# Attention buffers laid out by last use, and the last rows of v in four DMAs: a fused attention and spectral-mix kernel

## The chip, the cores and the metric

The kernel runs on one core of a Trainium2 chip. The metric is the device time of one execution in microseconds; the figure for the kernel before is the median of three runs.

## The reference

Two computations are chained. The first is sliding-window attention with ALiBi slopes over q, k, v of shape (8 batches, 8 heads, 576 positions, 64):

```python
scores = scale * np.matmul(q, k.transpose(0, 1, 3, 2))
mask = (rel >= 0) & (rel < 128)                # rel = query position - key position
scores = np.where(mask, scores + slopes * -abs(rel), -1e9)
x = softmax(scores) @ v                        # heads side by side: (8, 576, 512)
```

The second mixes x in the frequency domain with a full 512 x 512 complex matrix for each of 64 modes, and adds a channel projection:

```python
X = np.fft.rfft(x, axis=1)
Yr = einsum('bmd,mde->bme', Xr, w_r) - einsum('bmd,mde->bme', Xi, w_i)   # 64 modes
Yi = einsum('bmd,mde->bme', Xr, w_i) + einsum('bmd,mde->bme', Xi, w_r)
y = np.fft.irfft(Y, n=S, axis=1)
u = x + y
return u + np.maximum(u @ w_ch, 0.0)
```

All inputs are FP32. The 128 matrices of w_r and w_i are 134 MB, q, k and v together 28.3 MB.

## The kernel before

**Attention.** The work is cut into 16 units, one for each batch and group of four heads. Its order is written out by hand: the table `STAGE` lists 23 steps with a lag each, and the loop at L541 runs them for one stage after another, so that a stage holds the values of one unit, the scores of another and the casts of a third. For each unit, q, k and v arrive as FP32 in the tiles `qr`, `kr` and `vr`, which hold two units each; `cast` (L225) turns them to BF16 on VectorE (L233, L235 and L238), and at its end calls `load` for the unit two further on. `load` (L198) issues on SP's queue: for v four DMAs of 128 KB, one for each head (L208), and one of 64 KB for the last 64 positions of the four heads, 32 partitions wide (L212); for k and q one DMA of 576 KB each (L219). PE multiplies, ScalarE takes the exponentials into `att` and moves transposed q and k to `qkT`, VectorE masks, and `norm` (L339) divides the values into `x`.

**Semaphores of the DMAs.** The framework keeps eight outstanding DMAs of each kind: an issue on SP waits for the landing of the one eight places before it, and the same holds for the issues of GpSimd (POOL). In the trace, for instance, SP issues at 47.99 us after a landing at 47.97, and at 84.31 after one at 84.25.

**Weights.** GpSimd issues the loads of the weights with a cast to BF16 (512 KB as written for a matrix). Each goes to one of three homes:

- Fourteen matrices go to the pool `early`. From stage 1 to 13 one is let out in a stage, after a copy of one element of `x` (`gate`, L553) that waits for that stage's normalization.
- Seven go over the raw tiles `qr`, `kr` and `vr` as their last contents have been cast (`LATER`, L416 and L556; the issues are recorded at L459). How many in which stage is a small table.
- From L558 on the attention's own pools are closed, and six packs of two matrices go to the pool `wpool`, which lies over the memory that attention held (`load_packs`, L462, issued at L478). Its pack buffers, `YT` and the pool `fin` are laid out over the attention's tiles in the order in which they are allocated, so which tile a pack lies over decides what its DMA waits for. Before them, in GpSimd's order, stands a memset of a part of `YT` (L561).

After that, a matrix is loaded whenever a buffer is freed. The mixing (L858) takes four batches' worth of spectra against each weight; each group of four modes is then scaled (L596) and transposed to `YT`. The inverse transform, the projection and the output (L814 and the store after it) come at the end.

**Tiles of attention.** One pool, `afix`, holds `mask`, `bias`, the two `vb`, the two `vt`, the two `qkT` and the two `att`, in this order; `amid`, allocated before it, holds the cast `q` and `k` and the reciprocals `rec`. The index of `vb`, `vt`, `qkT` and `att` is the unit's number modulo two, so the ones numbered 1 are those of the last unit, 15.

Of the kernel before, what the change touches and what calls it, by code (L numbers as in the profile page):

```python
# [10 lines left out]
FP32 = mybir.dt.float32  # L11
BF16 = mybir.dt.bfloat16
# [8 lines left out]
P = 128  # L21
# [6 lines left out]
FULL = 4  # L28
# [4 lines left out]
W = D + 2  # L33

NC = 24


STAGE = (
# [8 lines left out]
class _Scratch:  # L47


    def __init__(self, ap):  # L50
        self.ap, self.used, self.tags = ap, 0, {}
# [55 lines left out]
class _Attention:  # L107


    def __init__(self, tc, ctx, q, k, v, consts, x, XC, raw):  # L110
        self.tc, self.nc = tc, tc.nc
        self.q, self.k, self.v = q, k, v
        self.ident, self.F, self.FT = consts
        self.x, self.XC = x, XC
        B, H, S, _ = q.shape
        self.S, self.NG = S, H // 4
        self.units = [(b, g) for b in range(B) for g in range(self.NG)]
        self.raw = raw
        self.mid = ctx.enter_context(tc.tile_pool(name="amid", bufs=2))
        self.ps = ctx.enter_context(tc.tile_pool(name="aps", bufs=1, space=PSUM))  # L120
        fix = ctx.enter_context(tc.tile_pool(name="afix", bufs=1))
        self.table = fix.tile([P, H, 2, 2 * P], BF16, name="mask")
        self.bias = fix.tile([P, H, 2, 2 * P], BF16, name="bias")
        self.vb = [fix.tile([P, 2, 4, 2, 2 * W], BF16, name=f"vb{i}") for i in range(2)]
        self.vt = [fix.tile([P, 4, 2, W], BF16, name=f"vt{i}") for i in range(2)]
        self.qkT = [fix.tile([P, 2, 2, (FULL + 1) * P], BF16, name=f"qkT{i}") for i in range(2)]
        self.att = [fix.tile([P, FULL * 8 * P + 64], BF16, name=f"att{i}") for i in range(2)]
        self.loaded, self.casted, self.open = {}, {}, {}

    def fixtures(self, i):  # L130
# [67 lines left out]
    def load(self, w, u):  # L198
        nc = self.nc
        if u >= len(self.units):  # L200
            return
        b, g = self.units[u]
        hs = slice(4 * g, 4 * g + 4)
        if w == "v":
            t = self.raw[w][:, u % 2]
            sv = self.v[b, hs]
            for h in range(4):
                nc.sync.dma_start(  # L208
                    out=t[:, :2, h],
                    in_=sv[h, : FULL * P].rearrange("(r p j) d -> p r (j d)", r=2, j=2),  # L210
                )
            nc.sync.dma_start(  # L212
                out=t[64:96, 2],
                in_=sv[:, FULL * P :].rearrange("h (p j) d -> p h (j d)", j=2),
            )
        else:
            t = self.raw[w][:, u % 2]
            src = (self.q, self.k)["qk".index(w)][b, hs]
            nc.sync.dma_start(  # L219
                out=t.rearrange("p e j d -> p e (j d)"),  # L220
                in_=src.rearrange("(e h) (p j) d -> (h p) e (j d)", h=2, j=TPP),
            )
        self.loaded[w, u] = t
# [115 lines left out]
    def norm(self, u, e):  # L339
        nc = self.nc  # L340
        b, g = self.units[u]
        av = self.open.pop(("av", e, u))
        cs = slice((4 * g + 2 * e) * D, (4 * g + 2 * e + 2) * D)
        rec = self.mid.tile([P, 2, FULL + 1], FP32, tag="rec")
        tiles = av[:, :, : (FULL + 1) * W].rearrange("p h (t n) -> p h t n", n=W)
        nc.vector.reciprocal(rec, tiles[:, :, :, D])
        nc.vector.tensor_tensor(  # L347
            out=self.x[:, b, :, cs].rearrange("p t (h d) -> p h t d", h=2),
            in0=tiles[:, :, :, :D],
            in1=rec.unsqueeze(-1).broadcast_to([P, 2, FULL + 1, D]),  # L350
            op=ALU.mult,
        )
        if b % 2 and g == self.NG - 1 and e == 1:

            nc.vector.tensor_copy(self.x[:64, b, FULL], self.x[:64, b - 1, FULL])
# [21 lines left out]
    def channels(self, u, _):  # L377
# [3 lines left out]
        if g < self.NG - 1:  # L381
            return
        xt = self.open.pop(("xt", u))
        NM = self.F.shape[2] // 2
        view = self.XC[:, : 4 * NC * NM].rearrange(
            "p (q s t b m) -> p q t s b m", q=2, s=3, t=2, b=8)[:, :, :, :, b]
# [13 lines left out]
def kernel(  # L400
# [10 lines left out]
    nc = tc.nc  # L411
# [1 line left out]
    B, H, S, _ = q.shape  # L413
    NM, DM, _ = moe_w_r.shape
    AHEAD = {stage: 1 for stage in range(1, 14)}
    LATER = {13: 2, 14: 2, 15: 3}  # L416
    EARLY, NWA, NWB, AGAIN = 14, 12, 4, 8
    HM = NM // 2

    const = ctx.enter_context(tc.tile_pool(name="const", bufs=1))  # L420
    x = const.tile([P, B, FULL + 1, DM], BF16, name="x")
    XC = const.tile([P, 4 * NC * NM + 16 * NM], BF16, name="XC")
    ident = const.tile([P, P], BF16, name="ident")
# [26 lines left out]
    def load_w(n, pool, chosen=None):  # L450

        for i in ([i for i in todo_w if i not in again][:n] if chosen is None else chosen):
            todo_w.remove(i)
            src = (moe_w_r, moe_w_i)[i % 2][i // 2].rearrange("(p a) e -> p a e", a=4)
            homes[i] = pool
            t = spare.pop(0) if pool is None else pool.tile([P, 4, DM], BF16, tag="w", name="w")
            for part in ((slice(0, 4),) if i < 2 * NM - 1
                         else (slice(0, 2), slice(2, 3), slice(3, 4))):
                nc.gpsimd.dma_start(out=t[:, part], in_=src[:, part])  # L459
            wq[i] = [t[:, a] for a in range(4)]  # L460

    def load_packs(n, pool):  # L462

        for _ in range(n):
            pack = [i for i in todo_w if i not in again][:2]
            if not pack:
                return
            assert len(pack) == 2
            t = pool.tile([P, 2, 4, DM], BF16, tag="w", name="w")
            kinds = {i % 2 for i in pack}  # L470
            for s, i in enumerate(pack):
                todo_w.remove(i)
                homes[i] = pool if s else False
                wq[i] = [t[:, s, a] for a in range(4)]
            m, w = pack[0] // 2, (moe_w_r, moe_w_i)
            if len(kinds) == 1:
                assert pack[1] == pack[0] + 2
                nc.gpsimd.dma_start(  # L478
                    out=t.rearrange("p s a e -> p s (a e)"),
                    in_=w[kinds.pop()][m : m + 2].rearrange("m (p a) e -> p m (a e)", a=4))  # L480
                continue
            for s, i in enumerate(pack):
                src = w[i % 2][i // 2].rearrange("(p a) e -> p a e", a=4)
                for part in ((slice(0, 4),) if i < 2 * NM - 1
                             else (slice(0, 2), slice(2, 3), slice(3, 4))):
                    nc.gpsimd.dma_start(out=t[:, s, part], in_=src[:, part])

    with ExitStack() as actx:
        at = _Attention(tc, actx, q, k, v, (ident, F, FT), x, XC, raw)
# [5 lines left out]
        def run(name, arg, u):  # L495
            if 0 <= u < n and (name, arg, u) not in done:
                done.add((name, arg, u))
                getattr(at, name)(u, arg)
# [6 lines left out]
        table = _forward_table(nc, pool, F, S)  # L505
        next(table)
        nc.vector.memset(norm, 2.0 / S)
        nc.vector.memset(norm[:32], 1.0 / S)
        for t in at.qkT:
# [5 lines left out]
        at.fixtures(1)  # L515
        nc.gpsimd.memset(XC[:, 4 * NC * NM :], 0.0)
        run("cast", "q", 0)
# [23 lines left out]
        for stage in range(min(lags), n + max(lags)):  # L541
            for name, arg, lag in STAGE:
                run(name, arg, stage - lag)
                if name in ("transpose", "exp") and side.get(stage):
                    for _ in range(1 + (name == "transpose")):
                        fn, h = side[stage].pop(0)
# [3 lines left out]
            if stage in AHEAD:  # L550
# [3 lines left out]
                load_w(AHEAD[stage], early)  # L554
            if stage in LATER:
                load_w(LATER[stage], None)  # L556

    with ExitStack() as mctx:  # L558
        fix = mctx.enter_context(tc.tile_pool(name="fix", bufs=1))
        YT = fix.tile([P, 2, 4, B, HM, 2], BF16, name="YT")  # L560
        nc.gpsimd.memset(YT[:, 1, :, :, HM - 4 :], 0.0)  # L561
        pool = mctx.enter_context(tc.tile_pool(name="fin", bufs=2))
        wctx = mctx.enter_context(ExitStack())
        wpool = wctx.enter_context(tc.tile_pool(name="w", bufs=NWA // 2, reuse_waits="tile"))
        again = todo_w[NWA : NWA + AGAIN]
        load_packs(NWA // 2, wpool)
        lctx, pctx = ExitStack(), ExitStack()
        lps = lctx.enter_context(tc.tile_pool(name="lps", bufs=1, side="right", space=PSUM))
        ps = pctx.enter_context(tc.tile_pool(name="fps", bufs=1, space=PSUM))
# [262 lines left out]
        for g in range(NM // 4):  # L832
# [5 lines left out]
            for i in range(8):  # L838
# [14 lines left out]
                for a in range(4):  # L853
                    for t in now:
                        m, ri = t // 2, t % 2
                        c0 = (a // 2 * 2 * NC + 16 * (1 - ri) + a % 2 * 8) * NM + m
                        into = part_acc if g == LAST and m < NM - 1 else acc
# [13 lines left out]
                if k == K1:  # L871
# [15 lines left out]
                    for b in range(2):  # L887
                        nc.gpsimd.dma_start(
                            out=FM.rearrange("(k v) b s -> k v b s", v=16)[:, b, b],
                            in_=FT[64 * b + 56 : 64 * b + 64, b, : 2 * P],  # L890
# [108 lines left out]
```

## Time and profile before

| | |
|---|---|
| median of three runs | 442.07 us (440.07 to 442.46) |
| profiled execution | 440.32 us |
| its span | 438.5 us (1.8 us lie around it) |
| mean granted clock of TensorE | 0.858 |
| busy: PE, VectorE, ScalarE, GpSimd | 73%, 42%, 37%, 20% of the span |
| read from HBM, written | 162.53 MB, 9.44 MB |
| packets of GpSimd's DMA queue | 18992, 67.22 MB as written |
| packets of SP's DMA queue | 33460, 37.79 MB |

Busy shares are means over the whole span. The page also cuts the span into 40 slices of 10.96 us, and gives for each the busy tenths of every engine, the share of time in which the 16 DMA engines worked (a mean over them; overlapping packets can push it a little over 1), and the rate in GB/s as written, so that a weight read in FP32 and written in BF16 counts half of what is read. An engine name with a q behind it (SPq, POOLq) is the queue of instructions of that engine. "A <- B" in a list of waits means that A stood idle until B was done, followed by the microseconds in all, the number of times, and the longest.

### The profile page before, as it was taken

Reading aid. Unit: us, or ns where it says so; the run is one execution under the profiler, and the core shown is the slowest. Engines: PE = TensorE matmul, PEld = TensorE weight load, DVE = VectorE, ACT = ScalarE, POOL = GpSimd, SP = SyncE. Lnnn points to the kernel's source line nnn. Section 1 sums busy time; section 2 is a strip of 40 time slices with the busy share of each in tenths; the row PEclk is TensorE's granted clock in tenths of the full one; section 3 lists DMA queues with packets and bytes.
Section 4 is the critical chain, followed back from the end, with each engine's and each line's share of the span. In section 5 each row is a group of like instructions: output and inputs, shape, how many; then the busy total and the mean of one; then the engine's idle time right before and its main releaser. Section 6 shows DMA issues by size and latency. Waiting matters only on the chain. (4 is left out here: it accounts for less than half of the span.)

```text
span 438.5 us, 8313 instructions
## 1 busy us (share of the span) xinstructions
PE 321.4 (73%) x3509; PEld 179.6 (41%) x3509; DVE 184.4 (42%) x332; ACT 162.1 (37%) x211; POOL 87.9 (20%) x162
## 2 busy tenths in 40 slices
PE   5689899979896534453442487999879999699982
PEld 4357677756665311111111133444434444233430
DVE  7799699987773301010000022322223232122684
ACT  6959799989680000000000012322232323101780
POOL 8711011101215001322112110111111110012500
PEclk9979899999899955555555569999999999989997
DMA  8999999999999999999999999999999999997597
GB/s 284 319 324 309 309 291 306 317 296 301 224 215 185 214 214 214 213 214 214 215 211 215 215 214 214 214 214 215 214 214 214 215 214 214 215 214 150 201 377 296
DMA packets 52489, 105.54 MB, mean 241 GB/s; under 512 B 4052, under 2 KB 23396, under 8 KB 52452
## 3 DMA queue, kind: packets, MB, share of 16 engines
q0 software_dynamic: 18992, 67.22, 76.9%
q1 hardware_dynamic: 33460, 37.79, 26.0%
q8 instruction: 27, 0.44, 0.4%
q14 instruction: 10, 0.08, 0.0%
HBM read 162.53 MB, written 9.44 MB: 392 GB/s over the span
## 5 line engine op out<-in xcount | busy, mean ns | idle before, releaser
L858 PE MATMUL acc<-w,XC 128*32 128x512 bf16 x456 | 79.6, 475 | 71.3 <-DMA w<-in_moe_w_i_dram 35.3
L858 PEld LDWEIGHTS <-XC 128*32 128x32 bf16 x508 | 38.5, 147 | 111.0 <-issue 83.8
L294 ACT ACTIVATE att<-sc 128x1024 bf16<-128x1024 f32 x64 | 64.0, 1032 | 10.6 <-PE sc L284 10.6
L624 ACT CAST ZW<-zw 128x512 bf16<-128x512 f32 x8 | 4.7, 585 | 145.1 <-PE zw L622 145.1
L331 PE MATMUL av<-vb,att 128*128 128x132 bf16 (+1 forms) x576 | 39.0, 219 | 11.2 <-DVE x L347 6.2
L596 DVE TENSOR_SCALAR yq<-acc 128x512 bf16<-128x512 f32 x14 | 9.6, 687 | 83.1 <-PE acc L858 83.1
L331 PEld LDWEIGHTS <-att 128*128 128x128 bf16 x704 | 37.2, 99 | 16.5 <-DVE x L347 10.4
L690 PE MATMUL my<-wch,xT 128*64 128x512 bf16 x288 | 34.5, 381 | 5.8 <-ACT x L721 4.3
L699 ACT CAST XW<-my 128x512 bf16<-128x512 f32 x36 | 19.3, 589 | 49.8 <-PE my L647 49.8
L671 DVE COPY xT<-tr 128x1024 bf16<-128x1024 bf16 x18 | 12.5, 692 | 54.3 <-PE tr L669 54.3
L256 ACT COPY qkT<-tp 128x1152 bf16<-128x1152 bf16 x30 | 33.5, 1116 | 2.4 <-PE tp L250 1.5
L478 POOL DMA_DIRECT2D w<-in_moe_w_i_dram x23 | 16.3, 708 | 66.8 <-PE acc L858 44.1
L478 POOL DMA_DIRECT2D w<-in_moe_w_r_dram x22 | 15.6, 709 | 65.9 <-PE acc L858 48.9
L347 DVE TENSOR_TENSOR x<-av,rec 128x640 bf16<-128x640 f32 x32 | 26.4, 825 | 1.1
L284 PE MATMUL sc<-qkT 64*64 64x256 bf16 (+2 forms) x640 | 25.2, 265 | 2.1 <-ACT qkT L256 1.2
L690 PEld LDWEIGHTS <-xT 128*64 128x64 bf16 x288 | 17.2, 109 | 21.6 <-issue 9.2
L814 DVE TENSOR_TENSOR o<-yy,r 128x1024 f32<-128x1024 f32 (+1 forms) x22 | 21.6, 1026 | 4.8 <-DMA Z<-yq 2.6
L553 POOL COPY gate<-x 1x1 bf16<-1x1 bf16 x13 | 6.3, 482 | 83.3 <-DVE x L347 83.3
L233 DVE CAST vb<-vr 64x1024 bf16<-64x1024 f32 x32 | 22.6, 707 | 0.2
L284 PEld LDWEIGHTS <-qkT 64*64 64x64 bf16 x640 | 14.6, 110 | 19.7 <-issue 16.7
L721 ACT CAST x<-my 128x512 bf16<-128x512 f32 x18 | 10.5, 585 | 32.0 <-PE my L647 32.0
L271 PE MATMUL sc<-bias,ident 128*128 128x512 bf16 x64 | 21.2, 415 | 1.4 <-ACT att L294 1.4
(134 smaller groups left out, 435.6 us busy)
## 6 DMA issues: line engine op xcount, KB each, us to landing
w<-in_moe_w_i_dram POOLq DMA_DIRECT2D x23, 1024.0 KB, 35.8
w<-in_moe_w_r_dram POOLq DMA_DIRECT2D x22, 1024.0 KB, 35.7
qr<-in_q_dram SPq DMA_DIRECT2D x16, 576.0 KB, 9.1
kr<-in_k_dram SPq DMA_DIRECT2D x16, 576.0 KB, 6.8
vr<-in_v_dram SPq DMA_DIRECT2D x64, 128.0 KB, 7.0
w<-in_moe_w_r_dram POOLq DMA_DIRECT2D x16, 512.0 KB, 14.3
w<-in_moe_w_i_dram POOLq DMA_DIRECT2D x13, 512.0 KB, 24.0
out_dram<-o SPq DMA_DIRECT2D x13, 512.0 KB, 4.6
```

The lines of the kernel that those rows point to most:

```text
L233: nc.vector.tensor_copy(self.vb[u % 2][row, :, :, :, W * half : W * half + D], src[row, :2])
L256: (self.nc.vector.tensor_copy if u < 2 and w == "q" else self.nc.scalar.copy)(dst.rearrange("q h (p j) -> q h p j", j=TPP), tp.rearrange(" ...
L271: nc.tensor.matmul(sc[:, e], lhsT=self.ident, rhs=self.bias[:, hv].rearrange("p j n -> p (j n)"), start=True, stop=False, skip_group_check ...
L284: nc.tensor.matmul(sc[64 * half : 64 * half + 64, e, j * 256 + c0 : j * 256 + c0 + n], lhsT=qkT[row, 1, h, k0 + j : k0 + P : 2], rhs=qkT[r ...
L294: self.nc.scalar.activation(self.att[u % 2][:, kt * 8 * P : (kt + 1) * 8 * P], sc.rearrange("p e n -> p (e n)"), AF.Exp, scale=1.0 / math. ...
L331: nc.tensor.matmul(bank[:, qt * W : qt * W + rhs[j].shape[1]], lhsT=att[:, o : o + P], rhs=rhs[j], start=(n == 0 and j == 0), stop=(n == l ...
L347: nc.vector.tensor_tensor(out=self.x[:, b, :, cs].rearrange("p t (h d) -> p h t d", h=2), in0=tiles[:, :, :, :D], in1=rec.unsqueeze(-1).br ...
L478: nc.gpsimd.dma_start(out=t.rearrange("p s a e -> p s (a e)"), in_=w[kinds.pop()][m : m + 2].rearrange("m (p a) e -> p m (a e)", a=4))
L690: nc.tensor.matmul(mm[ROWS[half]], lhsT=lhsT, rhs=wch[:, dt], start=(dt == 0), stop=False, skip_group_check=True,)
L699: nc.scalar.copy(XW[:, j, n], mms[n])
L814: nc.vector.tensor_tensor(out=o[:, c], in0=yy[:, c], in1=r[:, c], op=ALU.add)
L858: nc.tensor.matmul(into[32 * (m % 4) : 32 * (m % 4) + 32], lhsT=XC[:, c0 : c0 + 31 * NM + 1 : NM], rhs=wq[t][a], start=(ri == 0 and a == 0 ...
```

## The change

Three things are edited.

1. The attention's tiles are put into pools by the time of their last use. A pool `aend` at the bottom holds `att` and `vb` of odd units and both `vt`; a pool `asum` next to it holds `rec`; `afix` keeps `mask`, `bias`, both `qkT`, and `att` and `vb` of even units. `YT` and `fin` come to lie over `aend` and `asum`, and the packs over the cast q and k and over `afix`. The memset of `YT` moves behind the issues of the six packs. In the program that results, none of the six packs waits for the last normalization; the first waits for TensorE, the second for TensorE and ScalarE, the fifth for VectorE, and each for the landing of the DMA eight places before.
2. `LATER` lets one spare matrix out a stage earlier (one in stage 12, two in stage 15 in place of three); there are seven as before.
3. For units 1, 3, 5, 7, 9 and 11 the load of the last 64 positions of v is four DMAs of 8 partitions (16 KB each) in place of one of 32 partitions (64 KB). SP has 155 DMA issues in place of 137.

```diff
+EIGHTS = (1, 3, 5, 7, 9, 11)
...
+        end = ctx.enter_context(tc.tile_pool(name="aend", bufs=1))
+        self.sums = ctx.enter_context(tc.tile_pool(name="asum", bufs=2))
         self.mid = ctx.enter_context(tc.tile_pool(name="amid", bufs=2))
...
-        self.vb = [fix.tile([P, 2, 4, 2, 2 * W], BF16, name=f"vb{i}") for i in range(2)]
-        self.vt = [fix.tile([P, 4, 2, W], BF16, name=f"vt{i}") for i in range(2)]
         self.qkT = [fix.tile([P, 2, 2, (FULL + 1) * P], BF16, name=f"qkT{i}") for i in range(2)]
-        self.att = [fix.tile([P, FULL * 8 * P + 64], BF16, name=f"att{i}") for i in range(2)]
+        at = (fix, end)
+        self.att = [at[i].tile([P, FULL * 8 * P + 64], BF16, name=f"att{i}") for i in range(2)]
+        self.vb = [at[i].tile([P, 2, 4, 2, 2 * W], BF16, name=f"vb{i}") for i in range(2)]
+        self.vt = [end.tile([P, 4, 2, W], BF16, name=f"vt{i}") for i in range(2)]
...
-            nc.sync.dma_start(
-                out=t[64:96, 2],
-                in_=sv[:, FULL * P :].rearrange("h (p j) d -> p h (j d)", j=2),
-            )
+            tail = sv[:, FULL * P :].rearrange("h (p j) d -> p h (j d)", j=2)
+            step = 8 if u in EIGHTS else 32
+            for p0 in range(0, 32, step):
+                nc.sync.dma_start(out=t[64 + p0 : 64 + p0 + step, 2], in_=tail[p0 : p0 + step])
...
-        rec = self.mid.tile([P, 2, FULL + 1], FP32, tag="rec")
+        rec = self.sums.tile([P, 2, FULL + 1], FP32, tag="rec", name="rec")
...
-    LATER = {13: 2, 14: 2, 15: 3}
+    LATER = {12: 1, 13: 2, 14: 2, 15: 2}
...
-        nc.gpsimd.memset(YT[:, 1, :, :, HM - 4 :], 0.0)
         pool = mctx.enter_context(tc.tile_pool(name="fin", bufs=2))
...
         load_packs(NWA // 2, wpool)
+        nc.gpsimd.memset(YT[:, 1, :, :, HM - 4 :], 0.0)
```

## The prediction

> **What bounds the kernel now.** I first read the page's 40 slices. Each is 10.96 us of the span of 438.5 us.
>
> ```profile
> ## 2 busy tenths in 40 slices
> ...
> DMA  8999999999999999999999999999999999997597
> GB/s 284 319 324 309 309 291 306 317 296 301 224 215 185 214 214 214 213 214 214 215 211 215 215 214 214 214 214 215 214 214 214 215 214 214 215 214 150 201 377 296
> ```
>
> The DMA engines are full from the first microseconds to about 400 us. From slice 13 on they move 213 to 215 GB/s as written (the weights are read in FP32 and written in BF16, so twice that is read); one exception stands out, slice 12 with 185. The waits of TensorE from 170 to 400 us say who sets the pace there:
>
> ```profile
> PE acc L858 <- DMA w<-in_moe_w_r_dram: 30.3, 15, 3.0
> PE acc L858 <- DMA w<-in_moe_w_i_dram: 27.7, 13, 5.1
> ```
>
> TensorE waits 58 us for weights in 28 waits; the opposite wait is not the one that counts. So the end follows the weight stream: the last weight packets land near 402 us, and a tail of about 36 us comes behind them (the chain that ended last is a row of short steps). A microsecond in which the DMA engines stand empty anywhere before is a microsecond at the end, as long as all bytes must still come. One weight of 512 KB takes 524,288 B / 214 GB/s = 2.45 us. So I next looked for empty time in slice 12, in stretches of 1 to 4 us (the last two columns are DMA share and GB/s; a full stretch reads 1.06 and 213 to 214):
>
> ```profile
> 114.00:115.00 1.00, 1.00 (x12) 1.00 (x11) 0.97 (x3) 0.00 (x0) 0.00 (x0) 0.50 0.78 219
> 115.00:116.00 1.00, 1.00 (x9) 0.30 (x10) 1.00 (x3) 0.72 (x2) 0.63 (x2) 0.65 0.86 252
> 116.00:117.00 1.00, 1.00 (x23) 0.77 (x21) 0.44 (x1) 0.72 (x2) 1.00 (x3) 1.00 0.90 250
> 117.00:118.00 1.00, 1.00 (x20) 0.62 (x19) 0.00 (x0) 1.00 (x2) 1.00 (x3) 1.00 1.07 120
> 118.00:119.00 1.00, 1.00 (x23) 1.00 (x21) 0.09 (x1) 1.00 (x2) 0.46 (x1) 1.00 0.91 175
> 119.00:120.00 1.00, 0.94 (x23) 0.57 (x20) 0.97 (x3) 0.93 (x2) 0.00 (x0) 1.00 1.02 202
> ...
> 137.00:138.00 1.00, 0.66 (x12) 0.50 (x9) 0.00 (x0) 0.30 (x2) 1.00 (x2) 1.00 0.68 131
> 138.00:139.00 1.00, 0.00 (x0) 0.00 (x0) 0.62 (x2) 0.25 (x2) 1.00 (x3) 1.00 1.18 102
> 139.00:140.00 1.00, 0.84 (x8) 0.70 (x9) 0.00 (x0) 0.00 (x0) 1.00 (x2) 1.00 0.73 111
> ```
>
> There are two holes, at 114 to 120 and 137 to 140 us. What GpSimd, which issues the weights, was doing, shows why:
>
> ```profile
> 115.37 0.51 POOL L553 COPY gate<-x 1x1 bf16<-1x1 bf16 x1 [6.93 <-DVE x L347]
> ...
> 127.77 1.05 POOL L459 DMA_DIRECT2D vr<-in_moe_w_r_dram  x2 [5.66 <-DVE vb L233]
> 136.26 0.45 POOL L561 MEMSET YT<- 128x256 bf16 x1 [7.43 <-DVE x L347]
> 136.82 0.72 POOL L478 DMA_DIRECT2D w<-in_moe_w_i_dram  x1
> ```
>
> One weight per stage is let out behind a gate copy. The weight issued at 107.91 landed at 115.06, and the next was issued at 115.82. Later the queue holds what was issued up to 128.8, its last two landing at 136.66 and 139.29, while GpSimd stands 7.43 us at the memset of YT for the last normalization. The first pack is issued at 136.82: too late by its own start-up.
>
> **The change part by part.** *Layout and memset.* In the changed program the six packs no longer stand behind the memset, and their buffers lie over tiles used earlier. Packs 1 and 2 still wait for a last reader on TensorE or ScalarE, pack 5 for VectorE, and all for the landing of the weight eight places earlier. Those places are the weights that before landed from about 118 to 134 us, one per 2.45 us, so the queue stays eight deep. Packs may then go from about 129 instead of 136.8, against a queue that runs dry at 137: cover 8 us. Worth: (213-131 + 213-102 + 213-111)/213 = 1.38 us. Bounds: 0 (a pack's reader turns out to be the last stage) to 1.38. I take 1.38, the row itself. The memset (0.45 us) moves behind six issues of 0.72 us, 4.3 us; its reader is far later (the half it clears ends with the last modes), so nothing.
>
> *One spare weight a stage earlier.* It is issued near 108.4 behind the weight of 107.91, so one more 2.45 us stands in the queue when that lands at 115.06. Short of full at 114 to 117 are (0.28+0.20+0.16)/1.06 = 0.60 us by share; the slow restart at 117 to 120 lacks (93+38+11)/213 = 0.67 us. Bounds 0 and 1.27; I take 1.27, because the load of 2.45 us is longer than both, and hold the lower for the range: in these windows loads of the last values run too, and a standing weight queue may merely slow those.
>
> *The tails.* Of six units 64 KB go in four DMAs of 16 KB: 18 more issues on SP, 0.38 to 0.65 us each, 7 to 12 us of SP over 110 us, in which it mostly waits. Bytes and packet sizes (512 B, 27 to 30 ns) stay. What SP holds is eight outstanding DMAs: each issue waits for the landing of the one eight earlier. A unit now is ten DMAs, so in an odd unit the load of k waits for the landing of the same turn's first v load, and q for the second:
>
> ```profile
> 68.84 2.35 SPq L208 DMA_DIRECT2D vr<-in_v_dram  x4
> 71.29 0.41 SPq L212 DMA_DIRECT2D vr<-in_v_dram  x1
> 72.94 0.37 SPq L219 DMA_DIRECT2D kr<-in_k_dram  x1
> 74.61 0.95 SPq L219 DMA_DIRECT2D qr<-in_q_dram  x1
> ```
>
> The first v load of 68.84 landed at 76.84: k would go 3.9 us later than 72.94, and q at about 77.6, 3.0 us later; the v loads of 76.41 stand behind them. Does anything read late? k takes 6.8 us to land and its cast is 10 us after its issue: 3.2 us of cover. For q there is none late in attention:
>
> ```profile
> DVE q L238 <- DMA qr<-in_q_dram: 4.3, 3, 2.0
> SPq L208 <- DMA qr<-in_q_dram: 14.0, 11, 2.3
> ```
>
> The casts of q at 93.49, 100.97 and 108.55 start as its load lands. Yet a late issue is not a late landing: 6 to 10 us of latency are mostly queueing behind other loads, since a stage's bytes (1.77 MB of q, k, v and 1.05 MB read of one weight) at the 392 GB/s of the span are 7.2 us, which is the stage's period (casts of q 7.2 to 7.6 us apart). With fewer bytes outstanding the engines stay full and each load lands sooner. Bounds: 0 to 6.0 us (3.0 at each of the two units whose q has no cover, all of it lost). I take 0, since every row up to 114 reads full engines, and keep 6.0 for the range. *Spread:* should eight-row loads use half the engines, each of those has 6 x 8 x 28 ns = 1.34 us more and the others as much less; the last weight packets of the trace end between 401.0 and 402.5 us, so the engines are not level, and this is worth -1.34 to +1.34. Unknown sign: 0.
>
> The Trainium skill's page "DMA: Bandwidth & Descriptors", section "Rules for kernel authors", speaks against this part: small transfers should be made one large one, as under 64 KB one pays mostly overhead. [...] The same page ("Why a DMA increments its semaphore by 16 and not by 1") has an access pattern of 8 rows go to 8 engines, which would make the spread real and leave only its sign open; no run here shows it yet.
>
> **Sum.** 440.32 (profiled execution: span 438.5 and 1.8 around it) - 1.38 - 1.27 = 437.7. The median of the runs is 442.07, 1.75 above that execution, so in its terms 442.07 - 2.65 = 439.4. About 0.5% (2.2 us) is what a measurement of this kernel can tell from no change; the forecast is 0.6% faster.
>
> **Rivals.** *Slower: q comes late.* Mechanism as above: the slot of eight, at k and q of odd turns. It decides once the outstanding loads no longer fill the engines, so that the landing of q moves with its issue. Then attention, the gates and the weights all slip by 3.0 us at two units: 439.4 + 6.0 = 445.4; with a third unit, 448.4. For it: the casts that wait already and SP's 14.0 us behind q. Against it: full engines. *No difference:* the hole moves. The last two spare weights still wait for the last casts of v (5.66 us before 127.77); a standing queue slows the last v loads (the last tail of v before, issued at 115.5, landed at 121.03 among weights), and the gain at 114 to 120 is given back: 442.07 - 1.38 = 440.7; with neither hole filled 442.1. *The spread decides:* 438.1 or 440.7.
>
> **How the numbers follow.** Forecast, with the spread's good side, 0.45 (438.1 to 439.4); no difference, with the spread's bad side and half-gains, 0.17 (440.7 to 442.1); late q 0.38, of which a third only just beyond 0.5% and the rest around 445.4 to 448.4. Low end 436.6: both holes, the spread, and 1.5 us for scatter (442.07 - 2.65 - 1.34 = 438.1). High end 447.4 leaves out the worst of late q. The forecast's own range is 436.6 to 439.8.
>
> **What would show it.** Right: no stretch below a share of 1.0 from 108 to 145 us, packs issued before the memset and before 132 us, slice 12 at 213 or more, last weights 2 to 3 us earlier. Wrong: "DVE q L238 <- DMA qr" growing well beyond 4.3 us, SP waiting at L219 for v, GB/s in slices 3 to 10 below those shown, the last normalization later than 136.2 us.

## The result, and the profile after

The changed kernel takes 452.15 us (median of 6 runs, 451.01 to 453.30) against 440.90 for the kernel before on the same chip: a ratio of 1.0238, with an interval of 1.0215 to 1.0261. It is 2.4% slower, where 0.6% faster was forecast, and it lies above the forecast range. The profiled execution after has a span of 449.4 us. The same slices as before show where the time went:

```profile
DMA  8999899999996999999999999999999999999498
GB/s 281 295 303 297 237 273 278 261 301 285 277 234 119 214 213 214 214 213 215 215 212 213 213 215 214 215 215 215 214 214 215 214 214 214 215 213 176 167 378 310
```

A slice is now 11.2 us wide (10.96 before); counted from 0, slices 13 to 35 run at 212 to 215 GB/s, as they did (211 to 215). What is new lies ahead of them: slice 4 has fallen from 309 to 237 GB/s, slice 7 from 317 to 261, and slice 12, the one that was to be repaired, from 185 to 119. Two of the empty stretches, in steps of 1 us (the last two columns are DMA share and GB/s, and 1.06 is a full share):

```profile
49.00:50.00 1.00, 1.00 (x23) 0.80 (x23) 0.19 (x1) 1.00 (x2) 0.00 (x0) 1.00 0.64 140
50.00:51.00 1.00, 1.00 (x18) 0.58 (x19) 0.40 (x2) 0.73 (x1) 0.00 (x0) 1.00 0.12 32
51.00:52.00 1.00, 1.00 (x23) 0.76 (x19) 1.00 (x2) 0.57 (x1) 0.22 (x1) 1.00 0.64 85
...
140.00:141.00 1.00, 0.00 (x0) 0.00 (x0) 0.00 (x0) 0.00 (x0) 0.00 (x0) 0.57 0.47 95
141.00:142.00 1.00, 0.00 (x0) 0.00 (x0) 0.00 (x0) 0.00 (x0) 0.00 (x0) 0.50 0.15 39
142.00:143.00 1.00, 0.00 (x0) 0.00 (x0) 0.98 (x2) 0.00 (x0) 0.00 (x0) 0.50 0.00 0
143.00:144.00 1.00, 0.00 (x0) 0.00 (x0) 0.94 (x3) 0.00 (x0) 0.31 (x1) 0.50 0.00 0
144.00:145.00 1.00, 0.11 (x2) 0.11 (x3) 0.99 (x2) 0.00 (x0) 1.00 (x3) 0.50 0.31 16
145.00:146.00 1.00, 1.00 (x14) 1.00 (x14) 1.00 (x2) 0.00 (x0) 0.48 (x1) 0.50 0.36 57
```

The hole at 49 to 52 us did not exist before:

```profile
49.00:50.00 1.00, 1.00 (x15) 0.49 (x15) 1.00 (x2) 0.00 (x0) 0.19 (x1) 0.50 1.06 401
50.00:51.00 1.00, 1.00 (x10) 0.95 (x11) 1.00 (x3) 0.89 (x1) 0.85 (x2) 0.58 1.07 365
51.00:52.00 1.00, 1.00 (x20) 0.53 (x18) 0.55 (x1) 0.73 (x2) 0.00 (x0) 1.00 1.14 312
```

The hole at 140 to 146 us took the place of the one at 137 to 140. By the rate, as in the prediction, it costs (6 x 213 - 207) / 213 = 5.0 us in place of 1.4 (207 is the sum of its six rates).

The packets of the two traces, added up as bytes read (a weight's taken twice, as it is written in half of its bytes), tell when the time was lost. Before, the first 40 MB are in by 111.1 us; the changed kernel has them 9.2 us later. For 45 MB (125.5 us before) it is 7.6 us late, for 50 MB (137.3 us), the second hole by then behind it, 12.8 us, and from 55 MB on it stays 11.4 to 11.5 us late. So most of the loss comes before the second hole, and the weight stream behind it makes up for nothing.

**The first kind of loss** is to be read on SP's queue. This is the turn that loads unit 9 (start, length, line):

```profile
76.17 2.98 SPq L213 DMA_DIRECT2D vr<-in_v_dram  x4
79.24 5.01 SPq L220 DMA_DIRECT2D vr<-in_v_dram  x4
85.42 0.39 SPq L224 DMA_DIRECT2D kr<-in_k_dram  x1
85.90 0.41 SPq L224 DMA_DIRECT2D qr<-in_q_dram  x1
86.41 2.91 SPq L213 DMA_DIRECT2D vr<-in_v_dram  x4
```

The four small loads stretch over 5.01 us, because each waits for the landing of the DMA eight places earlier. For the third that is the k of the turn before, for the fourth its q: in the trace the third goes at 80.82 us, after that k's landing at 80.81, and the fourth at 83.98, after that q's landing at 83.97. Then k goes, when the turn's first load of v has landed (85.35). From 10 to 130 us, SP's waits for a q at the loads of v's last rows (L220) and for v's loads at k and q (L224) are:

```profile
SPq L220 <- DMA qr<-in_q_dram: 11.2, 5, 2.9
SPq L224 <- DMA vr<-in_v_dram: 4.7, 5, 2.1
```

The issue of k comes 9.25 us after the first issue of v (85.42 - 76.17), where before it came 4.1 us after (72.94 - 68.84). At that moment the eight DMAs ahead of k are four of 128 KB and four of 16 KB: 576 KB in all, which is an estimated 1.5 us of work at the 392 GB/s of the span before. The first of them took 9.2 us to land (76.17 to 85.35), so SP cannot keep the engines filled. Before, the eight DMAs ahead of k were four and one of v's, and a k, a q and a v load of the turns before: 4 x 128 + 64 + 2 x 576 + 64 KB, some 1.8 MB. VectorE feels it (from 10 to 160 us):

```profile
DVE vb L238 <- DMA vr<-in_v_dram: 11.0, 3, 8.9
DVE q L243 <- DMA qr<-in_q_dram: 7.1, 5, 2.0
DVE k L243 <- DMA kr<-in_k_dram: 6.5, 4, 2.1
```

Before, only q was late in this stretch:

```profile
DVE q L238 <- DMA qr<-in_q_dram: 5.7, 4, 2.0
```

The last cast of q has moved from 108.5 to 115.8 us.

**The second kind of loss** is in the 8.9 us of the first row, and in what GpSimd does behind it:

```profile
129.53 0.54 POOL L464 DMA_DIRECT2D vr<-in_moe_w_i_dram  x1 [4.12 <-DMA vr<-in_v_dram]
143.69 1.06 POOL L464 DMA_DIRECT2D vr<-in_moe_w_r_dram  x2 [13.63 <-DVE vb L238]
144.73 0.75 POOL L483 DMA_DIRECT2D w<-in_moe_w_i_dram  x1
...
152.50 0.31 POOL L571 MEMSET YT<- 128x256 bf16 x1 [1.37 <-PE av L336]
```

The packs no longer wait for the memset. But they stand behind two spare weights that go over the v buffers; these wait for the last cast of v, and that begins at 142.0 us instead of 126.1. SP came to the last loads of v from 120.6 to 122.7 us, with six weights put on GpSimd's queue between 116.5 and 125.4. The queues from 132 to 140 us (packets, MB, share of the engines' time):

```profile
q0 software_dynamic: 445, 1.62, 100.8%
q1 hardware_dynamic: 169, 0.08, 4.8%
```

0.08 MB in 8 us is 10 GB/s for the loads that attention waits for, beside weights that nobody needs yet. The rest comes through as the weight queue runs dry, near 141 us; then the engines stand empty until v is cast and the next weights are issued.

### The profile page after: what moved, and what is told of

Same layout as the page of the kernel before. It is cut to its first block, busy times and chain, and to the rows that moved or that the text cites. A ratio compares the mean times of both kernels' runs of the same rounds, so it can differ in the third digit from the quotient of the medians.

```text
span 449.4 us, 8341 instructions
## 1 busy us (share of the span) xinstructions
PE 324.4 (72%) x3509; PEld 182.2 (41%) x3509; DVE 184.0 (41%) x332; ACT 162.5 (36%) x211; POOL 87.6 (19%) x162
## 5 line engine op out<-in xcount | busy, mean ns | idle before, releaser
L336 PE MATMUL av<-vb,att 128*128 128x132 bf16 (+1 forms) x576 | 41.0, 225 | 25.5 <-DVE x L352 20.7
L336 PEld LDWEIGHTS <-att 128*128 128x128 bf16 x704 | 39.4, 103 | 31.2 <-DVE x L352 23.3
L238 DVE CAST vb<-vr 64x1024 bf16<-64x1024 f32 x32 | 22.7, 710 | 11.4 <-DMA vr<-in_v_dram 11.0
```

The source lines that it names most:

```text
L238: nc.vector.tensor_copy(self.vb[u % 2][row, :, :, :, W * half : W * half + D], src[row, :2])
L336: nc.tensor.matmul(bank[:, qt * W : qt * W + rhs[j].shape[1]], lhsT=att[:, o : o + P], rhs=rhs[j], start=(n == 0 and j == 0), stop=(n == l ...
```

## The experiments

Twelve kernels were run, in the groups in which they appear here. "Last q" and "last v" are the times at which the last cast of each begins in the profiled execution (108.5 and 126.1 us before; 115.8 and 142.0 after). That is one execution of several: for e6 the fastest (440.05 us), for e8 the second fastest (442.00), for e5 and e10 the slowest (448.06 and 443.47). The ratio is the recorded one, not the quotient of two medians.

| kernel | median, us | ratio to before (interval) | last q | last v |
|---|---|---|---|---|
| the whole change | 452.15 | 1.0238 (1.0215-1.0261) | 115.8 | 142.0 |
| e1: the change, no small loads | 439.62 | 1.0000 (0.9963-1.0037) | 109.8 | 127.3 |
| e2: before, with the small loads | 447.76 | 1.0159 (1.0123-1.0195) | 115.7 | 133.2 |
| e3: the change, old spare table | 446.96 | 1.0133 (1.0064-1.0202) | 114.9 | 131.1 |
| e4: layout and memset alone | 439.53 | 0.9961 (0.9938-0.9983) | 108.4 | 124.6 |
| e5: e3, four small loads by head | 446.77 | 1.0108 (1.0055-1.0160) | 115.9 | 134.2 |
| e6: e3, v heads in two loads | 442.83 | 1.0029 (0.9998-1.0059) | 109.6 | 125.9 |
| e7: e4, v heads in two loads | 439.76 | 0.9965 (0.9944-0.9986) | 109.7 | 127.4 |
| e8: e4, spare weights earlier | 444.75 | 1.0060 (1.0033-1.0086) | 108.7 | 132.4 |
| e9: e3, units 1, 3, 5 only | 443.87 | 1.0051 (1.0031-1.0071) | 113.8 | 130.0 |
| e10: e6, small loads by head | 440.81 | 0.9984 (0.9967-1.0002) | 113.5 | 131.3 |
| e11: e7, spare weight earlier | 439.52 | 0.9965 (0.9936-0.9994) | 110.1 | 126.3 |
| e12: the change, v heads in two loads | 441.26 | 1.0008 (0.9976-1.0039) | 112.3 | 128.6 |

### Taking the change apart: e1 to e4

Theory A says that the eight slots are at fault, theory B that the spare weight let out earlier is. e1 is the change without its small loads:

```diff
-EIGHTS = (1, 3, 5, 7, 9, 11)
+EIGHTS = ()
```

> The change without its four small loads (new layout, memset behind the packs, one spare weight a stage earlier). Theory A (slots: eight outstanding DMAs on SP, ten instead of seven DMAs in a turn, k and q late): the loss was in the small loads, so this gains what the prediction summed for the rest: 438 to 440 us. Theory B (trap: the spare weight let out a stage earlier makes a standing queue of weights, behind which the last loads of v crawl): the last cast of v is late here too, after 132 us, and the time is 444 us or more.

e2 is the kernel before with the new `load` and `EIGHTS` only.

> The kernel before with the four small loads in six units, nothing else. Theory A: all of the loss is here: 447 to 452 us, with the same empty stretches of the DMA engines at 12 to 16 and 48 to 52 us as in the changed kernel. Theory B: 440 to 442 us, no difference.

e3 is the change with the spare weights as before:

```diff
-    LATER = {12: 1, 13: 2, 14: 2, 15: 2}
+    LATER = {13: 2, 14: 2, 15: 3}
```

> The changed kernel with the spare weights let out as before (2, 2, 3 from stage 13 on). Theory A: the loss stays but for the hole at the end of attention: 447 to 451 us. Theory B: the trap is gone, the last cast of v is on time: 441 us or less.

e4 takes both edits, so only the layout and the memset are left.

> The kernel before with the new layout and the memset behind the packs, nothing else. Both theories: the hole of 1.38 us at 137 to 140 us is filled and nothing else moves: 439 to 440 us, against 441 for the kernel before. If the packs' own waits take the place of the memset: 441.

The medians are 439.62, 447.76, 446.96 and 439.53. The small loads cost 7.4 us with the new layout (e3 against e4) and 6.6 with the old one (e2 against the 441.2 of before in the same comparison), so theory A holds for the larger part; in e2 the engines' share is 0.87 from 12 to 16 us and 0.74 from 48 to 52, as A had said, where it was 1.08 and 1.07 before. The four runs of e2 lie within 0.7 us, those of e3 spread from 443.0 to 449.4, so that sizes taken from e3 are good to a few us only. The spare weight costs nothing by the median where attention is on time (e1 against e4), and 5.2 us where the small loads have made it late (452.15 against e3, the lowest of its six runs being 451.0). That is an interaction that neither theory had foreseen: e3 left 447 as A said, but A gave no reason for the 452. The layout gives what was forecast. In e4 the packs go out from 127.3 to 135.1 us, ahead of the memset at 135.77, and the stretch that held the hole of 1.38 us is full:

```profile
137.00:138.00 1.00, 0.34 (x2) 0.23 (x4) 0.40 (x2) 0.00 (x0) 0.00 (x0) 0.50 1.11 221
138.00:139.00 1.00, 1.00 (x8) 0.44 (x5) 0.00 (x0) 0.00 (x0) 0.00 (x0) 0.50 1.12 225
139.00:140.00 1.00, 1.00 (x10) 0.53 (x9) 0.00 (x0) 0.00 (x0) 0.15 (x1) 0.50 1.01 205
```

Its ratio of 0.9961 is 1.7 us of 441.2 (0.8 to 2.7 by the interval), beside the 1.38 of the sum.

### Slots, or eight partitions: e5 and e6

A small load differs from the old one in two ways: there are more of them, and each is 8 partitions wide. e5 keeps the number and makes them 32 wide:

```diff
-            for p0 in range(0, 32, step):
-                nc.sync.dma_start(out=t[64 + p0 : 64 + p0 + step, 2], in_=tail[p0 : p0 + step])
+            if u in EIGHTS:
+                for h in range(4):
+                    nc.sync.dma_start(out=t[64:96, 2, h], in_=tail[:, h])
+            else:
+                nc.sync.dma_start(out=t[64:96, 2], in_=tail)
```

> New layout, spare weights let out as before, and in the six units the last rows of v in four DMAs of 32 partitions, one for each head: as many DMAs and bytes as with 8 partitions, which took 447.0 us. Theory A (slots): the number of DMAs is what costs, so 446 to 448 us again, and q is cast last near 115 us instead of 108. Theory C (the 8 partitions: half of the engines carry these loads, so that a load lands late): four full-width loads cost nothing, 439 to 441 us, last cast of q near 108.

e6 keeps the width and gives slots back, in the same six units:

```diff
+            if u in EIGHTS:
+                for r in range(2):
+                    nc.sync.dma_start(
+                        out=t[:, r],
+                        in_=sv[:, 2 * P * r : 2 * P * r + 2 * P].rearrange(
+                            "h (p j) d -> p h (j d)", j=2),
+                    )
-            for h in range(4):
+            for h in range(4) if u not in EIGHTS else ():
```

> The same with the loads of 8 partitions, but in these six units the heads of v come in two DMAs of 256 KB instead of four of 128 KB: eight DMAs a turn instead of ten, with the small loads unchanged. Theory A: k and q of such a turn no longer wait for the turn's own v, so most of the 7 us comes back: 440 to 442 us. Theory C: the small loads are the same, so 446 to 448 us.

e5 takes 446.77 us, the same as 8 partitions (446.96), with the last cast of q at 115.9. Its engines stand nearly empty after one of the six turns, for instance, in the same way:

```profile
82.00:83.00 1.00, 1.00 (x22) 0.87 (x22) 0.97 (x3) 0.27 (x1) 0.00 (x0) 0.81 0.21 57
83.00:84.00 1.00, 1.00 (x20) 0.49 (x18) 1.00 (x2) 1.00 (x2) 0.42 (x1) 1.00 0.13 30
84.00:85.00 1.00, 1.00 (x24) 1.00 (x25) 1.00 (x3) 1.00 (x2) 0.69 (x2) 1.00 0.27 53
```

e6, with ten DMAs brought down to eight, falls to 442.83, its last cast of q is back at 109.6, and the hole at 49 to 52 us is gone:

```profile
49.00:50.00 1.00, 1.00 (x19) 0.58 (x19) 0.39 (x2) 0.74 (x1) 0.00 (x0) 1.00 1.01 351
50.00:51.00 1.00, 1.00 (x23) 0.77 (x22) 1.00 (x2) 0.56 (x1) 0.22 (x1) 1.00 1.03 391
51.00:52.00 1.00, 1.00 (x20) 0.62 (x19) 1.00 (x3) 1.00 (x2) 0.83 (x2) 1.00 1.05 383
```

Of the 7.4 us, 4.1 come back (446.96 to 442.83), with the small loads unchanged. So it is the count against the eight slots that costs most; the width does not explain the 7.4 us. The two profiles overstate the contrast, as the one of e5 is of its slowest run and the one of e6 of its fastest, and 3.3 us over e4 remain.

### Fewer loads still, and the trap by itself: e7 and e8

e7 uses two loads for the heads of v in all units, and no small ones: five DMAs a turn.

> The new layout alone (439.5 us) with the heads of v in two DMAs in all units and no small loads: five DMAs a turn instead of seven. Theory A, drawn the other way: SP's waits for earlier landings shrink (14 us behind q before), q is issued earlier and its casts wait less, the last cast of q before 108 us: 437 to 439 us. If eight outstanding loads already suffice where the units have seven: 439 to 440 us.

It takes 439.76 us, no less than e4 with seven. SP's waits for the landing of a q have shrunk from 14.0 us in e4 (11 waits) to 1.0 (one), but attention is no earlier (last q 109.7): the second expectation. Here, where the engines were already full, more bytes in flight bought nothing.

e8 lets spare weights out earlier still, without any small load:

```diff
-    LATER = {13: 2, 14: 2, 15: 3}
+    LATER = {11: 1, 12: 2, 13: 1, 14: 1, 15: 2}
```

> The new layout alone with spare weights let out earlier still (1 in stage 11, 2 in 12, 1 in 13, 1 in 14, 2 in 15). Theory B (a standing queue of weights traps the last loads of v, small loads or not): the last two casts of v wait for their loads, the last of them after 130 us, an empty stretch of the DMA engines follows, and the time is 443 us or more. If the trap needs attention to be late already: 438 to 440 us.

The median is 444.75 us. The casts of q are on time (last 108.7), but the last cast of k begins at 118.9 in place of 113.3 in e4, after a wait of 3.8 us for its load, and the last cast of v at 132.4. The engines stand empty just then:

```profile
132.00:133.00 1.00, 1.00 (x19) 0.97 (x17) 0.59 (x1) 0.05 (x1) 0.00 (x0) 1.00 0.32 68
133.00:134.00 1.00, 1.00 (x17) 0.37 (x14) 0.99 (x3) 0.93 (x3) 0.00 (x0) 1.00 0.02 4
134.00:135.00 1.00, 0.71 (x14) 0.26 (x12) 0.94 (x3) 1.00 (x2) 0.91 (x2) 1.00 0.00 0
```

GpSimd had waited 7.54 us for that cast before it could issue the next weights:

```profile
134.09 1.06 POOL L464 DMA_DIRECT2D vr<-in_moe_w_r_dram  x2 [7.54 <-DVE vb L238]
```

The trap needs no small loads. In both cases the last loads of v were issued behind several standing weights; the change reached this by making v late, e8 by making the weights early.

### Where the small loads cost, and whether the whole is explained: e9 to e12

e9 is e3 with `EIGHTS = (1, 3, 5)`.

> New layout, spare weights as before, and the four small loads in units 1, 3 and 5 only (with all six it took 447.0, with none 439.5). The prediction's rival priced only the two late units, whose q has no cover, at 3.0 us each, and the early ones at nothing: then 439 to 440 us. If every such turn costs about the same, the slots empty the DMA engines early too (they stood half empty at 12 to 14 and 49 to 53 us): half of 7.4, so 442.5 to 444 us.

It takes 443.87 us: 4.3 of the 7.4 us by the medians, 4.0 of 7.6 by the ratios, come from the first three units, so about half. The hole at 49 to 52 us is there, and deeper:

```profile
49.00:50.00 1.00, 0.85 (x8) 0.37 (x7) 0.50 (x2) 0.18 (x1) 0.00 (x0) 0.50 0.22 59
50.00:51.00 1.00, 0.79 (x15) 0.62 (x16) 1.00 (x2) 0.02 (x1) 0.32 (x1) 0.50 0.07 18
51.00:52.00 1.00, 1.00 (x11) 0.83 (x9) 1.00 (x3) 1.00 (x1) 0.72 (x2) 0.64 0.63 88
```

e10 is e6 with its small loads taken by head, as in e5.

> Eight DMAs in the six units' turns (heads of v in two), with the last rows of v in four DMAs of 32 partitions, one for each head, in place of four of 8 partitions. With 8 partitions this took 442.8 us, 3.3 above the layout alone. If those 3.3 are the spread over the engines that the prediction left open, they go: 439 to 440.5 us. If they are the number of DMAs, they stay: 442 to 444 us.

It takes 440.81 us, between the two expectations and 2.0 below e6. Against e5, which has the same small loads, giving the slots back is worth 6.0 us (446.77 to 440.81). From e6 to e10, the intervals (0.9967 to 1.0002 and 0.9998 to 1.0059) barely touch, and the two were compared with different runs of the kernel before (medians 441.62 and 441.36). Some 2 us can be the spread over the engines; that it is so isn't shown, and with ten DMAs a turn the same exchange made 0.2 us (e3 and e5).

e11 is e7 with the change's table of spare weights.

> The new layout with the heads of v in two DMAs in all units (439.8 us) and one spare weight a stage earlier. The hole at 114 to 118 us, which that kernel still shows, is filled: by the prediction's term 1.27 us less, 438.5 us, if attention keeps its time. If the standing weight slows the last loads of v by as much, as it seems to have with four DMAs: 439 to 440.5 us.

It takes 439.52 us against 439.76, the second expectation: the spare weight is worth nothing by the median. Three of its twelve runs took 443.8 to 444.7 us, two of the ten of e1 took 444.1 to 444.3 and three of the twelve of e12, with the same table, 444.8 to 445.4, where none of the ten of e4 or e7 took more than 441.4. That the trap closes now and then with this table would fit, but none of those runs was profiled.

e12 is the whole change, with the heads of v in two loads in the six units, as in e6.

> The whole change (452 us) with one thing undone: in the six units the heads of v come in two DMAs, so that a turn has eight instead of ten. With the spare weights let out as before that took 442.8 us. Theory A, whole: the slots made attention late, and only late attention meets the standing weights of the earlier spare load, so both losses go: 440 to 443 us, last cast of v before 129 us. Theory B alone: the earlier spare load traps the last loads of v whenever it comes with the small loads: 445 us or more, last cast of v after 132 us.

It takes 441.26 us, 10.9 below the change, with its last cast of v at 128.6 and these waits of VectorE for loads:

```profile
DVE q L250 <- DMA qr<-in_q_dram: 8.0, 6, 2.2
...
DVE k L250 <- DMA kr<-in_k_dram: 1.5, 1, 1.5
DVE vb L245 <- DMA vr<-in_v_dram: 0.3, 1, 0.3
```

The wait for v has gone from 11.0 to 0.3 us, though the spare weight still goes out a stage early. With the slots given back, both losses go, but for 1.7 us against e4. No version that was run beats the layout alone (e4, 439.53) by more than the measurement can tell.

## Why the prediction was wrong

**The term that failed** is "The tails": bounds of 0 to 6.0 us, of which 0 was taken "since every row up to 114 reads full engines". It measured 7.4 us with the new layout and 6.6 with the old one, beyond the upper bound. A wait had been named: k and q behind the turn's own v. A longer one had not: the small loads behind the q of the turn before (11.2 us in five waits, against 4.7 for the one that was named). But the error that set the term to 0 was in the next step, that "with fewer bytes outstanding the engines stay full and each load lands sooner". The full share of before was kept up by what was in flight, and the change takes just that away: four of the eight slots now hold 16 KB. The sum that was missing is the one above: 576 KB in flight is 1.5 us of work, beside loads that take 9 us to land. A busy share of the kernel before says nothing of a change to the thing that keeps it busy.

**The size of the rival "q comes late"** was near (6.0 us, or 9.0 with a third unit), but its place was wrong. It counted two late units whose q has no cover; e9 shows about half of the cost in units 1, 3 and 5, which it had priced at nothing. What is lost there is engine time, not cover, and the rival's own "decides once the outstanding loads no longer fill the engines" was the right point, priced in the wrong units.

**One spare weight a stage earlier** was taken at 1.27 us of gain, with 0 as the other bound. It is 0 by the median (e1 against e4), though the hole at 114 to 120 us is filled in e1 (shares of 1.02 to 1.23, against 0.73 to 1.09 from 114 to 120 in e4). The last v of e1 is 2.7 us later than in e4; that attention so pays back what the weights gain fits, but is not shown. And with late attention it costs 5.2 us. The prediction had the mechanism ("a standing queue slows the last v loads") and the row for it, a tail of 64 KB that took 5.5 us to land among weights, but priced it only as a gain given back. It can be more than that: the v buffers are what the next weights wait for, so a trapped load of v empties the very queue that traps it. The small loads alone bring the time to the edge of the range (446.96 and 447.76, against its high end of 447.4); together with the spare weight they took it 4.8 us beyond.

**Right** were the layout and the memset (1.7 us by e4's ratio for 1.38 in the sum) and the packs' own waits, which hide under the queue of eight when attention is on time.

**The spread** over the engines, -1.34 to +1.34, stays open; e6 and e10 allow some 2 us and settle no sign. What it supposed, that a load of 8 rows uses half of the engines, does fit the counts of packets under 512 B: 4052 before, 4148 in e3, 4340 in e5. They come out if a load of 32 rows adds 16 such packets and one of 8 rows 8 (24 x 8 - 6 x 16 = 96, and 24 x 16 - 6 x 16 = 288). The times that the prediction gave for the last weight packets (401.0 to 402.5 us) were misread as well: in the trace of before the last weight load lands at 404.3.

**Small transfers.** The Trainium skill's page "DMA: Bandwidth & Descriptors", section "Rules for kernel authors", would have small transfers made one, and the runs side with it. Its reason, that under 64 KB one pays mostly overhead, is at most a small part of what they show: e5 and e10 have the very same small loads, and differ by 6.0 us through the other loads of the turn.

## What to carry to other kernels

Where a queue keeps a fixed number of DMAs outstanding, a small DMA takes the place of a large one: before splitting a load, add up the bytes that remain in flight and divide by the rate. Where that came to 1.5 us against loads that took 9 us to land, the engines emptied, however full they had been. A load that is needed soon should not be issued behind a standing queue of loads that are not, least of all when these wait for the buffer that it fills. And two edits that are each harmless or mild should be priced together when one moves the time at which the other begins.

## What the runs showed of the hardware

With weights standing on GpSimd's queue, the loads of SP's queue got 10 GB/s of 215 in the changed kernel from 132 to 140 us (169 packets beside 445, mostly of 512 B against 4096). From 126 to 128 us, with weights standing as well, 512-byte packets of SP's queue alone made 221 GB/s. So loads of v got next to nothing beside weights at one time and most of the engines at another; what decides between the two is not shown.
